# Two MoE layers behind a delta-rule attention: first loads reordered, expert 0 staged elsewhere, first pair split, order lists drawn

## The chip, the cores and the metric

One NeuronCore of a Trainium2 chip (trn2) runs the whole program. The metric is device time in microseconds (us) of that core. TensorE (PE) multiplies matrices, with weight loads (PEld) beside it; VectorE (DVE), ScalarE (ACT) and GpSimd (POOL) do the rest; the sync engine's queue (SP) issues nearly all transfers, which run on 16 DMA engines.

## The reference, cut to what matters

```python
def _attn_ref(q, k, v, beta):
    k_n = k / (np.linalg.norm(k, axis=-1, keepdims=True) + 1e-06)
    for t in range(S):
        y[:, :, t] = np.einsum('bhd,bhde->bhe', q[:, :, t], state)
        v_old = np.einsum('bhde,bhd->bhe', state, kt)
        state = state + bt[:, :, :, None] * np.einsum('bhd,bhe->bhde', kt, vt - v_old)

def _moe_ref(x, w_gate, w1, w2):
    P = np.exp(logits - logits.max())
    for _ in range(8):
        P /= P.sum(1, keepdims=True) + 1e-09
        P /= P.sum(0, keepdims=True) + 1e-09
        P *= N / E
    for e in range(E):
        out += P[:, e:e + 1] * (np.maximum(x @ w1[e], 0.0) @ w2[e])
```

Attention is a delta rule over 768 steps for 4 batches of 8 heads of 48. Its output, 3072 tokens of 384, goes through a dense MoE layer (8 experts, 384 to 1024 to 384, each token weighted by a Sinkhorn-normalised matrix), and then through a second MoE layer in which each token goes to one expert only.

## The kernel before, in words

Attention is done in 24 blocks of 64 steps (`block(i)`, L517; block i is chunk i // 2 of batch pair i % 2). A block loads its keys and queries (`KQ`) and values in node `ld` (L561 to L566), squares and normalises the keys (L568 to L605), inverts a triangular 64x64 matrix per head in five levels `z`, `a` (L673 to L687), applies the running state (L710 to L757) and writes its output, split into a high and a low f16 half and transposed, into a ring `xring` (nodes `px`, `xe`, L796 to L806). Every f32 operand is split in that way, and each product takes three f16 matmuls.

Two blocks give 256 tokens, on which `moe_unit(e, r)` (L828) runs expert 0, and half of expert 1, of the first MoE layer: a first layer (L851), relu and split (L862, L864), a second layer (L877) and a store through `yo` (L887). Unit (0, r) has 72 matmuls of 256 columns and 48 of 384; unit (1, r) has half of each. `seq` fixes the order of the units: (0,0), (0,1), (1,0), (0,2), (1,1) and so on. A unit's first matmul waits for the output of both its blocks and for the end of the unit before.

Weights come as f32 and are split on the chip by `prep_nodes` (L911): loads `wl` (L933), a Square over them on ACT to find a scale (`wa`, L946), and the splits `we` on ACT (L984) and `wf` on DVE (L986). Expert 0 is staged in `xring` before the ring has data: first `w1` in three loads; then, when all its splits are done, `w2` in one load to the same place. The gate weights have a chain of their own (`wg0` to `wg`, L1035 to L1051). Zero tiles for the block-diagonal operands of the first blocks are loaded from HBM (L1059).

What sets the order of all this is a planner, `Sched` (L45). Every piece of work is a node with an engine, a cost, dependencies and a priority; `run` (L91) simulates the engines and issues at each step the ready node that can start first, the lowest priority number first among those that can. A result counts as seen on another engine `HOP` ns later (3000 for a DMA, plus the node's `lat`); `floor` is the earliest time of a node in the simulation. Each engine then works through its list strictly in that order. A node's priority in a block is `fpr`, i minus a lead (L432, L559); block 2's front has -1, block 3's 0, block 1's 1. The last stage (routing, and the second MoE layer's queue) is ordered by the same class.

One `KQ` buffer serves all blocks but block 1, whose keys lie in `hhl`; so `ld` of block i waits until block i-1 has used its keys (block 2: block 0):

```python
N("ld", "D", 1300, f, [("kl", pb), ("ql", pb), ("kn", pb), P4("r2l"), P4("sqv")]
  if i > 1 else [("cs", 0), ("wl02", 0)] if i else [])
```

After the attention stage PE goes on with the other experts (from L1263), then routing, then the second MoE layer.

Of the kernel before, what the change touches and what calls it, by code (L numbers as in the profile page):

```python
# [7 lines left out]
F32 = mybir.dt.float32  # L8
# [36 lines left out]
class Sched:  # L45
    HOP = {"P": 200.0, "V": 135.0, "A": 150.0, "G": 100.0, "D": 3000.0}
# [4 lines left out]
    SLACK = 300.0  # L51

# [38 lines left out]
    def run(self):  # L91
        ready = [n for n in self.nodes if n.wait == 0]
        left = len(self.nodes)
        while left:
            best = None
            per = {}
            for n in ready:
                opt = None
                for e, c_ in n.alts:
                    s = self.start(n, e)  # L100
                    if s is None:
                        continue
                    w = s + c_ + (self.BIAS.get(e, 0.0) if not n.one else 0.0)
                    if opt is None or w < opt[3]:
                        opt = (s, e, c_, w)
                if opt:
                    per.setdefault(opt[1], []).append((opt[0], n.prio, n, opt[2]))
            for e, cs_ in per.items():
                lim = max(self.free[e], min(x[0] for x in cs_)) + 1.0
                if e == "P":  # L110
                    mo = [x for x in cs_ if x[2].moe]
                    at = [x for x in cs_ if not x[2].moe]
                    if mo and at:
                        adv = self.free["P"] - self.tlast
                        self.tlast = self.free["P"]
                        self.credit = min(self.credit + adv * SH0, 1500.0)
                        ta = min(x[0] for x in at)
                        tm = min(x[0] for x in mo)
                        now = self.free["P"]
                        cs_ = mo if (self.credit >= 400 and tm <= max(now, ta) + 50) or (ta > now + 100 and tm < ta - 50) else at  # L120
                        lim = max(self.free[e], min(x[0] for x in cs_)) + 1.0
                x = min((y for y in cs_ if y[0] <= lim), key=lambda y: (y[1], y[0]))
                if best is None or x[0] < best[0]:
                    best = (x[0], e, x[3], x[2])
            s, e, c_, n = best
            if e == "P":
# [18 lines left out]
            n.fn(*args)  # L145
            end = s + c_
            self.free[e] = end
            self.log.append((n.name, e, s, end))
            if n.holder is not None:
                h = n.holder  # L150
                h.left -= 1
                h.fin = max(h.fin, end + self.FREE)
                if h.left == 0:
                    self.slots[h.ps[0]][h.slot] = h.fin
            ready.remove(n)
            left -= 1
            for m in n.out:
                m.wait -= 1
                same = e == "P" and m.one and m.alts[0][0] == "P"
                slack = self.SLACK + self.TOP[e] if m.one and m.alts[0][0] == "P" and not same else 0.0  # L160
                m.ready = max(m.ready, end + (0.0 if same else self.HOP[e]) + n.lat + slack)
                if m.wait == 0:
                    ready.append(m)


@with_exitstack
def kernel(
# [58 lines left out]
    lg = res.tile([128, NT, E], F32, name="lg")  # L226
# [18 lines left out]
    P = P9[:, :, 0:E]  # L245
    pet = res.tile([128, E + 1, NT], F32, name="pet")
# [188 lines left out]
    LP, AP, SP = 0.03, 0.7, 1.7  # L435
# [6 lines left out]
    with (  # L442
# [74 lines left out]
        def block(i):  # L517
# [21 lines left out]
            def front(name, shape, dt, at):  # L539
# [266 lines left out]
            N("xe", (("A", 690), ("V", 480)), 0, f, ["px", "W0", ("W1a", i // 4), ("mo", (i // 2) - NXR), ("x1", i - 2 * NXR - 1 + i % 2)], frees="px", prio=tp)  # L806
# [21 lines left out]
        def moe_unit(e, r):  # L828
# [13 lines left out]
            XR = xring[:, r % NXR]  # L842
            for g4 in range(nf // per):
                for j in range(per):
                    f_ = per * g4 + j
                    for kk in range(KD):
                        def f(slot=None, g4=g4, j=j, f_=f_, kk=kk):
                            if j == 0 and kk == 0:
                                o[g4] = ps1.tile([128, 512], F32, name="pt")
                            for x, (wv, xv) in enumerate(((0, 0), (0, 1), (1, 0))):  # L850
                                nc.tensor.matmul(  # L851
                                    out=o[g4][:, 256 * j:256 * j + 256], lhsT=w1v(W, wv, kk, f_), rhs=XR[:, xv, kk],
# [7 lines left out]
                        N(nm, "P", 327, f, dep, ps=("pt", 1) if j == 0 and kk == 0 else None, cols=768, moe=True)  # L860
# [7 lines left out]
            for j, t_ in enumerate(blks):  # L868

                spare = j % 2 and t_ >= NT - 5  # L870
                for f_ in range(nf):
                    def f(slot=None, j=j, f_=f_, spare=spare):
                        if f_ == 0:
                            o["py", j] = pyt(slot if spare else None)
                        c_ = 256 * (f_ % per) + 128 * j
# [35 lines left out]
        def prep_nodes(e, W, st, prio, deps, wdeps, hf=None, iv=None, fro=True):  # L911
# [5 lines left out]
            for x, wsrc in enumerate((moe_w1, moe_w2)):  # L917
                o = {}
                so = 0
                if hf is None:  # L920
# [9 lines left out]
                else_ = deps[x] if hf is not None and (x == 0 or so) else pv  # L930
                lof = {}
                for n_, (cs_, dst, src) in enumerate(loads):
                    Q((f"wl{x}{n_}", iv), "D", 650, lambda dst=dst, src=src: nc.sync.dma_start(out=dst, in_=src),  # L933
                      deps[n_] if x == 0 and hf is None else else_, prio[x][0], lat=1500.0 if len(cs_) < NCH else 4500.0, floor=4500.0)
                    for c in cs_:
                        lof[c] = (f"wl{x}{n_}", iv)
                if fro:

                    wd_ = 1024 if hf is None else 768
                    np_ = len(cks) * CW // wd_  # L940
                    for n_ in range(np_):
                        def f(n_=n_, o=o, so=so, x=x, wd_=wd_, np_=np_):
# [3 lines left out]
                            nc.scalar.activation(out=jk, in_=st[:, so + n_ * wd_:so + n_ * wd_ + wd_], func=AF.Square, accum_out=o["mx"][:, n_:n_ + 1])  # L946
# [34 lines left out]
                for n_, c in enumerate(cks):  # L981
                    a, b = so + n_ * CW, so + n_ * CW + CW
                    h_, l_ = (W[:, wcol(x, c, part):wcol(x, c, part) + CW] for part in range(2))
                    Q((f"we{x}{n_}", iv), "A", 520, lambda a=a, b=b, h_=h_, o=o: nc.scalar.activation(  # L984
                        out=h_, in_=st[:, a:b], func=AF.Copy, scale=o["s"]), [(f"wd{x}", iv)] + wdeps[x], prio[x][2])
                    Q((f"wf{x}{n_}", iv), "V", 602, lambda a=a, b=b, h_=h_, l_=l_, o=o: nc.vector.scalar_tensor_tensor(  # L986
                        out=l_, in0=st[:, a:b], scalar=o["s"], in1=h_, op0=ALU.mult, op1=ALU.subtract), [(f"we{x}{n_}", iv)], prio[x][2])
# [47 lines left out]
        Q(("wg0", 0), "D", 650, lambda: nc.sync.dma_start(out=wg_s, in_=moe_w_gate.rearrange("(k p) e -> p k e", p=128)), [("bt2", 0)], 0.6)  # L1035
# [5 lines left out]
        Q(("wg1", 0), "V", 90, f, [("wg0", 0)], 0.6)  # L1041

        pmax("wg2", 0, lambda: wgo["m"], wgo, 0.6, [("wg1", 0)])
# [4 lines left out]
        Q(("wg3", 0), "V", 700, f, [("wg2", 0)], 0.6)  # L1048
        Q(("wg4", 0), "A", 220, lambda: nc.scalar.activation(out=wgh, in_=wg_s, func=AF.Copy, scale=wgo["s"]), [("wg3", 0)], 0.6)
        Q(("wg", 0), "V", 150, lambda: nc.vector.scalar_tensor_tensor(  # L1050
            out=wgl, in0=wg_s, scalar=wgo["s"], in1=wgh, op0=ALU.mult, op1=ALU.subtract), [("wg4", 0)], 0.6)  # L1051
# [14 lines left out]
        w0a, w0 = prep_nodes(0, W0, xring.rearrange("p r a k n -> p (r a k n)").bitcast(F32), [(LP, AP, SP), (WP, WP, WP)], [[]] * 3, [[], []])  # L1066
# [7 lines left out]
        for i in range(NT):  # L1074
            block(i)
            if i % 2:
# [59 lines left out]
        sch.run()  # L1136
# [678 lines left out]
```

## Time and profile before

| | |
|---|---|
| three timed runs | 2177.27 us median (2176.48 to 2181.3) |
| the profiled execution | 2180.33 us, span 2178.6 us |
| mean granted clock of PE | 0.975 |
| PE / DVE / ACT / POOL busy | 2040.0 / 1217.7 / 837.5 / 265.6 us |
| MoE weight loads into `st`, the largest group of transfers | 28 of 1536 KB |

Times in the rows are us from the start of the span. "Idle before" is the time that the engine stood still just before an instruction, with what ended it. A granted clock of 1.00 is PE's upper level, 0.50 the lower. One execution was profiled; the runs of the table were timed without a profile.

### The profile page before, as it was taken

The numbers are of one execution on the slowest core, as the hardware profiler recorded it, in microseconds if no ns is written. First come the engines' busy times: TensorE is split into PE (matmuls) and PEld (weight loads), VectorE is DVE, ScalarE is ACT, GpSimd is POOL, SyncE is SP. The second block draws the span as 40 slices with busy tenths as digits, with TensorE's granted clock in tenths as the row PEclk, the third lists the DMA queues.
The fourth block names the chain that finished last, engine by engine and source line by source line (L and its number), as shares of the span: only waits on it lengthen the run. The fifth ranks groups of instructions, "written<-read, shape, count | busy, mean of one in ns | idle before, by whom it ended". The sixth has DMA issues, their size and how long they took to land. (4 is left out here: it accounts for less than half of the span.)

```text
span 2178.6 us, 45252 instructions
## 1 busy us (share of the span) xinstructions
PE 2040.0 (94%) x18968; PEld 1290.2 (59%) x18968; DVE 1217.7 (56%) x2777; ACT 837.5 (38%) x1568; POOL 265.6 (12%) x301
## 2 busy tenths in 40 slices
PE   3689988988998989999999999999999999999999
PEld 3567777777775435555555555555555555557776
DVE  6889888877872564555455455554552245552111
ACT  6666655565542332232222222222231135443332
POOL 3232233222200000000000000000000000113221
PEclk9589999999999999999999999999999999999999
DMA  7345555555534233113203113212300001058765
GB/s 263 85 100 110 118 108 102 113 110 105 131 100 167 95 99 116 59 59 116 87 30 116 59 65 110 88 48 99 116 30 1 1 16 29 23 187 318 253 235 205
DMA packets 328321, 232.51 MB, mean 107 GB/s; under 512 B 258908, under 2 KB 305920, under 8 KB 321714
## 3 DMA queue, kind: packets, MB, share of 16 engines
q1 hardware_dynamic: 322674, 217.76, 34.1%
q0 software_dynamic: 4288, 10.25, 1.3%
q8 instruction: 150, 2.46, 0.5%
q10 hardware_dynamic: 1152, 1.57, 0.2%
q14 instruction: 57, 0.47, 0.1%
HBM read 148.51 MB, written 51.93 MB: 92 GB/s over the span
## 5 line engine op out<-in xcount | busy, mean ns | idle before, releaser
L355 PE MATMUL pt<-big,W 128*128 128x512 f16 x2304 | 507.1, 380 | 9.4 <-DVE hhl L339 5.8
L355 PEld LDWEIGHTS <-W 128*128 128x128 f16 x2304 | 225.9, 98 | 280.6 <-issue 14.9
L366 PE MATMUL py<-W,hhl 128*128 128x384 f16 x1632 | 286.8, 327 | 4.1 <-DVE accb L385 3.9
L366 PE MATMUL py<-W,ttb 128*128 128x384 f16 x1440 | 253.6, 326 | 0.0
L338 ACT ACTIVATE hhl<-pt 128x512 f16<-128x512 f32 x136 | 81.1, 596 | 412.8 <-PE pt L355 412.1
L366 PEld LDWEIGHTS <-hhl 128*128 128x128 f16 x1632 | 160.0, 98 | 115.0 <-issue 6.7
L366 PEld LDWEIGHTS <-ttb 128*128 128x128 f16 x1440 | 140.9, 98 | 93.1
L385 DVE SCALAR_TENSOR_TENSOR accb<-py,pet,accb 128x384 f32<-128x384 f32 x136 | 83.9, 617 | 185.9 <-PE py L366 184.2
L851 PE MATMUL pt<-xring,W 128*128 128x256 f16 x1296 | 177.7, 275 | 0.5 <-DVE hhl L864 0.5
L339 DVE SCALAR_TENSOR_TENSOR hhl<-pt,hhl 128x512 f16<-128x512 f32 x136 | 93.9, 690 | 147.5 <-ACT hhl L338 147.4
L877 PE MATMUL py<-W,hhl 128*128 128x384 f16 x756 | 152.9, 331 | 6.3 <-ACT yo L887 3.8
L339 DVE SCALAR_TENSOR_TENSOR ttb<-pt,ttb 128x512 f16<-128x512 f32 x120 | 83.0, 691 | 108.4 <-ACT ttb L338 108.4
L338 ACT ACTIVATE ttb<-pt 128x512 f16<-128x512 f32 x120 | 71.6, 597 | 151.4 <-PE pt L355 151.4
L298 DVE TENSOR_REDUCE wmx<-st 128x1 f32<-128x512 f32 x168 | 109.8, 677 | 33.9 <-DMA st<-in_moe_w_dram 33.9
L305 POOL PARTITION_ALL_REDUCE wma<-wm x28 | 10.1, 362 | 945.5 <-DVE wm L303 945.5
L851 PEld LDWEIGHTS <-W 128*128 128x128 f16 x1296 | 114.7, 99 | 15.3 <-issue 0.6
L1327 PEld LDWEIGHTS <-W 128*128 128x128 f16 x1008 | 91.1, 98 | 53.7 <-issue 2.6
L1347 PE MATMUL py<-W,hhl 128*128 128x384 f16 x624 | 108.8, 326 | 0.0
L877 PEld LDWEIGHTS <-hhl 128*128 128x128 f16 x864 | 76.0, 99 | 46.9 <-issue 5.9
L1327 PE MATMUL pt<-big,W 128*128 128x512 f16 x432 | 97.6, 379 | 1.4 <-DVE hhl L1333 1.2
L1333 DVE SCALAR_TENSOR_TENSOR ttb<-pt,ttb 128x512 f16<-128x512 f32 x50 | 34.6, 692 | 111.5 <-ACT ttb L1332 111.1
L502 DVE TENSOR_TENSOR Z<-pz,cs 128x512 f16<-128x512 f32 x120 | 80.3, 674 | 10.3 <-PE pz L488 9.9
(373 smaller groups left out, 3094.0 us busy)
## 6 DMA issues: line engine op xcount, KB each, us to landing
st<-in_moe_w_dram SPq DMA_DIRECT2D x28, 1536.0 KB, 9.6
W<-w2d SPq DMA_DIRECT2D x18, 1536.0 KB, 8.7
w2d<-big SPq DMA_DIRECT2D x16, 1536.0 KB, 6.2
big<-w2d SPq DMA_DIRECT2D x8, 1536.0 KB, 7.1
accb<-w2d SPq DMA_DIRECT2D x8, 1536.0 KB, 8.4
big<-kqc SPq DMA_DIRECT2D x90, 128.0 KB, 3.8
KQ<-in_kq_dram SPq DMA_DIRECT2D x23, 448.0 KB, 4.8
st<-PTc SPq DMA_DIRECT2D x42, 128.0 KB, 2.7
```

The source lines that it names most:

```text
L298: nc.vector.tensor_reduce(out=mx[:, c:c + 1], in_=st[:, c * CW:c * CW + CW], op=ALU.max, axis=AX.X, apply_absolute_value=True)
L338: nc.scalar.activation(out=oh, in_=pt, func=AF.Relu)
L339: nc.vector.scalar_tensor_tensor(out=ol, in0=pt, scalar=0.0, in1=oh, op0=ALU.max, op1=ALU.subtract)
L355: nc.tensor.matmul(out=po, lhsT=lhsT, rhs=rhs, start=(i == 0), stop=(i == 3 * KD - 1))
L366: nc.tensor.matmul(out=py[:, 0:DM], lhsT=lhsT, rhs=rhs, start=(n == 0), stop=(n == 3 * (KF - fs) - 1))
L385: nc.vector.scalar_tensor_tensor(out=acc[t], in0=py[:, 0:DM], scalar=pe[x][:, t:t + 1], in1=acc[t], op0=ALU.mult, op1=ALU.add)
L502: ENG[e].tensor_tensor(out=out, in0=in0, in1=in1, op=op)
L851: nc.tensor.matmul(out=o[g4][:, 256 * j:256 * j + 256], lhsT=w1v(W, wv, kk, f_), rhs=XR[:, xv, kk], start=(kk == 0 and x == 0), stop=(kk = ...
L877: nc.tensor.matmul(out=o["py", j][:, 0:DM], lhsT=a_[f_ // per][:, c_:c_ + 128], rhs=w2v(W, b_, f_), start=(f_ == 0 and x == 0), stop=(f_ = ...
L1327: nc.tensor.matmul(out=po, lhsT=w1v(W, wv, kk, f), rhs=xv[:, kk, :], start=(kk == 0 and x == 0), stop=(kk == KD - 1 and x == 2))
L1333: V((f"rs{q_}", id_), lambda q_=q_: nc.vector.scalar_tensor_tensor(out=HL[q_], in0=o[q_], scalar=0.0, in1=HH[q_], op0=ALU.max, op1=ALU.sub ...
L1347: nc.tensor.matmul(out=o["py"][:, 0:DM], lhsT=a_[f // per][:, c_:c_ + 128], rhs=w2v(W, b_, f), start=(f == 0 and x == 0), stop=(f == KF - ...
```

## The change

The loads of the first blocks are moved in SP's list: block 1's waits for the constants only, block 3 gets a key buffer that is free from the start (two `KQ` buffers, by the block's parity), and from block 4 on `ld` waits for block i-2. Expert 0's `w1` loads get a later floor (9 us in the simulation) and a lower priority; its `w2` is staged in two halves in the parts of expert 1's tile `W1` that hold nothing yet, so it doesn't wait for the splits of `w1`. Block output into the ring waits for the splits of `w1` only. The first pair of blocks is given to the MoE layer as two units of one block (128 columns each). The gate weights' chain gets priority 1.4. The logits `lg` are written into the tile of the probabilities. The planner separates the plan from the issue, draws 40 plans with shuffled priorities, replays each six times with random delays (`late`), and issues the best; its DMA hop is 3400. The last stage's `run()` draws once.

```diff
@@
-    HOP = {"P": 200.0, "V": 135.0, "A": 150.0, "G": 100.0, "D": 3000.0}
+    HOP = {"P": 200.0, "V": 135.0, "A": 150.0, "G": 100.0, "D": 3400.0}
+    SHUFFLE = 0.2
-    def run(self):
+    def run(self, draws=1):
+        base = [(n.prio, n.wait, n.ready) for n in self.nodes]
...
+        for k in range(draws):
+            rng = random.Random(k)
+            for n, (p, w, r) in zip(self.nodes, base):
+                n.prio, n.wait, n.ready = p + (self.SHUFFLE * (rng.random() - 0.5) if k and p < 1e5 else 0.0), w, r
...
+            order = self.plan()
+            if order is None:
+                continue
+            end = sum(self.late(order, random.Random(j)) for j in range(6)) if draws > 1 else 0.0
+            if best is None or end < best[0]:
+                best = (end, order, self.log)
...
+    def late(self, order, rng):
...
+                if de != "P" or e != "P":
+                    t += self.HOP[de] + d.lat + 80.0 * rng.random() + (1000.0 * rng.random() ** 2 if de == "D" else 0.0)
...
+            elif rng.random() < 0.06:
+                c_ += 200.0 + 400.0 * rng.random()
...
+        return max(free.values())
+
+    def plan(self):
...
-    lg = res.tile([128, NT, E], F32, name="lg")
+    lg = P
...
-    LP, AP, SP = 0.03, 0.7, 1.7
+    LP, AP, SP = 0.35, 0.7, 1.7
...
-                return tl(name, shape, dt, 0)
+                return tl(name, shape, dt, key)
...
-                t = front("KQ", [896], F32, 0)
+                t = front("KQ", [896], F32, 0, par)
-            N("ld", "D", 1300, f, [("kl", pb), ("ql", pb), ("kn", pb), P4("r2l"), P4("sqv")] if i > 1 else [("cs", 0), ("wl02", 0)] if i else [])
+            N("ld", "D", 1300, f, ([] if i == 3 else [("kl", i - 2), ("ql", i - 2), ("kn", i - 2)]) + [P4("r2l"), P4("sqv")] if i > 1 else [("cs", 0)] if i else [], lat=500.0, **(dict(prio=0.15) if 0 < i < 3 else {}))
...
-            N("xe", (("A", 690), ("V", 480)), 0, f, ["px", "W0", ("W1a", i // 4), ("mo", (i // 2) - NXR), ("x1", i - 2 * NXR - 1 + i % 2)], frees="px", prio=tp)
+            N("xe", (("A", 690), ("V", 480)), 0, f, ["px", ("W0a", 0), ("W1a", i // 4), ("mo", (i // 2) - NXR), ("x1", i - 2 * NXR - 1 + i % 2)], frees="px", prio=tp)
...
-        def moe_unit(e, r):
+        def moe_unit(e, r, only=None):
...
-            blks = [2 * r, 2 * r + 1]
+            blks = [2 * r, 2 * r + 1] if only is None else [2 * r + only]
+            nt_ = 128 * len(blks)
+            c0 = 128 * (only or 0)
...
-            per = 2
+            per = 512 // nt_
...
-            XR = xring[:, r % NXR]
+            XR = xring[:, r % NXR, :, :, c0:c0 + nt_]
...
-                        N(nm, "P", 327, f, dep, ps=("pt", 1) if j == 0 and kk == 0 else None, cols=768, moe=True)
+                        N(nm, "P", 327 if nt_ == 256 else 170, f, dep, ps=("pt", 1) if j == 0 and kk == 0 else None, cols=3 * nt_, moe=True)
...
-                        (cks, st.rearrange("p (k f) -> p k f", k=KF), wsrc[e].rearrange("(k p) f -> p k f", p=128))]
+                        (cks[KD * u:KD * u + KD], st1[u].rearrange("p (k f) -> p k f", k=FH), wsrc[e][512 * u:512 * u + 512].rearrange("(k p) f -> p k f", p=128))
+                        for u in range(2)]
...
-                else_ = deps[x] if hf is not None and (x == 0 or so) else pv
+                else_ = deps[x] if hf is not None and (x == 0 or so) else pv if st1 is None else []
...
-                      deps[n_] if x == 0 and hf is None else else_, prio[x][0], lat=1500.0 if len(cs_) < NCH else 4500.0, floor=4500.0)
+                      deps[n_] if x == 0 and hf is None else else_, prio[x][0], lat=1500.0, floor=9000.0 + 6000.0 * x)
...
-        Q(("wg0", 0), "D", 650, lambda: nc.sync.dma_start(out=wg_s, in_=moe_w_gate.rearrange("(k p) e -> p k e", p=128)), [("bt2", 0)], 0.6)
+        Q(("wg0", 0), "D", 650, lambda: nc.sync.dma_start(out=wg_s, in_=moe_w_gate.rearrange("(k p) e -> p k e", p=128)), [("bt2", 0)], 0.5, lat=4000.0)
...
-        w0a, w0 = prep_nodes(0, W0, xring.rearrange("p r a k n -> p (r a k n)").bitcast(F32), [(LP, AP, SP), (WP, WP, WP)], [[]] * 3, [[], []])
+        w0a, w0 = prep_nodes(0, W0, xring.rearrange("p r a k n -> p (r a k n)").bitcast(F32), [(LP, AP, SP), (LP, AP, WP)], [[]] * 3, [[], []],
+                             st1=[W1[:, 6144 * u:6144 * u + 3072].bitcast(F32) for u in range(2)])
...
-            if i % 2:
+            if i < 2:
+                moe_unit(0, 0, i)
+            elif i % 2:
                 moe_unit(0, i // 2)
...
-        sch.run()
+        sch.run(40)
```

## Rows read from the trace of the kernel before

**Rows 1.** The page's 40 slices of the span, busy tenths.

```profile
PE   3689988988998989999999999999999999999999
...
DVE  6889888877872564555455455554552245552111
```

**Rows 2.** Windows: stretch, length, busy PE PEld DVE ACT POOL, PEclk, DMA, GB/s.

```profile
0.00:160.00 160.00, 95.89 (x1662) 82.42 (x1664) 125.90 (x328) 106.31 (x224) 50.31 (x52) 0.80 0.56 148
160.00:620.00 460.00, 421.87 (x7883) 335.74 (x7880) 380.09 (x880) 269.31 (x563) 123.03 (x109) 0.98 0.54 112
620.00:720.50 100.50, 91.36 (x614) 59.06 (x612) 38.81 (x104) 25.40 (x45) 1.34 (x6) 0.95 0.37 128
720.50:2178.00 1457.50, 1430.88 (x8822) 813.01 (x8819) 672.92 (x1466) 436.45 (x737) 90.89 (x134) 0.99 0.28 99
```

**Rows 3.** Timeline (start, length, engine): Sinkhorn's end, the next stage's first matmuls.

```profile
659.11 0.24 DVE L426 TENSOR_SCALAR pet<-pet,ivt 128x24 f32<-128x24 f32 x1
...
720.50 4.05 PE L355 MATMUL pt<-big,W 128*128 128x512 f16 x18
```

**Rows 4.** Windows inside the first 124 us.

```profile
10.00:20.00 10.00, 4.93 (x46) 4.71 (x46) 4.40 (x10) 5.12 (x9) 1.45 (x2) 1.00 1.02 334
20.00:30.00 10.00, 1.81 (x26) 1.63 (x27) 3.83 (x13) 6.30 (x15) 1.15 (x1) 1.00 0.78 266
...
80.00:124.00 44.00, 31.58 (x641) 28.47 (x641) 37.41 (x92) 29.73 (x61) 13.75 (x12) 0.61 0.37 75
```

**Rows 5.** Timeline of SP, the first 42 us.

```profile
10.79 0.33 SPq L564 DMA_DIRECT2D KQ<-in_kq_dram  x1
...
15.31 5.69 SPq L1059 DMA_DIRECT2D ttb<-in_zer_dram  x1
...
21.52 0.48 SPq L564 DMA_DIRECT2D hhl<-in_kq_dram  x1
...
41.19 0.38 SPq L933 DMA_DIRECT2D xring<-in_moe_w_dram  x1
```

**Rows 6.** Timeline, 20 to 28 us; idle before in brackets.

```profile
20.87 0.63 ACT L577 ACTIVATE K<-KQ 128x512 f16<-128x512 f32 x1 [5.69 <-DMA KQ<-in_kq_dram]
...
23.91 0.18 DVE L1040 TENSOR_REDUCE wm<-wg_s 128x1 f32<-128x24 f32 x1 [5.74 <-DMA wg_s<-in_moe_w_gate_dram]
...
26.09 0.52 ACT L570 ACTIVATE K<-hhl 128x384 f32<-128x384 f32 x1 [2.77 <-DMA hhl<-in_kq_dram]
...
27.85 0.59 PE L488 MATMUL pz<-t,W 128*128 128x64 f16 x8 [9.90 <-ACT W L506]
```

**Rows 7.** DMA, first 50 us: packets; zero fills, KB, us to landing.

```profile
DMA packets 9807, 14.01 MB, mean 280 GB/s; under 512 B 4940, under 2 KB 6732, under 8 KB 9804
...
big<-in_zer_dram SPq DMA_DIRECT2D x9, 512.0 KB, 9.1
```

**Rows 8.** Timeline of PE: output of blocks 0 and 1, first MoE matmuls.

```profile
79.20 0.83 PE L799 MATMUL px<-c,yhl 128*128 128x128 f16 x6
...
122.25 0.49 PE L799 MATMUL px<-c,yhl 128*128 128x128 f16 x6 [0.41 <-DVE mx L780]
...
124.24 1.80 PE L851 MATMUL pt<-xring,W 128*128 128x256 f16 x15
```

**Rows 9.** Timeline of PE: matmuls of 128, 256 and 384 columns.

```profile
140.67 1.50 PE L657 MATMUL pg<-kqc,big 128*128 128x128 f16 x24
...
648.68 4.09 PE L851 MATMUL pt<-xring,W 128*128 128x256 f16 x36
...
658.10 4.06 PE L877 MATMUL pz<-W,hhl 128*128 128x384 f16 x24
```

**Rows 10.** Waits, 160 to 620 us: total us, times, longest.

```profile
ACT K L570 <- DMA KQ<-in_kq_dram: 26.9, 14, 5.0
...
DVE ss L582 <- ACT K L570: 12.5, 8, 4.0
...
PE sv L592 <- DVE ss L584: 5.7, 3, 3.7
```

More of the change, by code (lines that the diff above doesn't have):

```diff
@@ L1 @@
+import random
 from contextlib import ExitStack
@@ L89, in start @@
         return s
-    def run(self):
+    def run(self, draws=1):
+        base = [(n.prio, n.wait, n.ready) for n in self.nodes]
+        free, slots = dict(self.free), {k_: list(v) for k_, v in self.slots.items()}
+        best = None
+        for k in range(draws):
+            rng = random.Random(k)
+            for n, (p, w, r) in zip(self.nodes, base):
+                n.prio, n.wait, n.ready = p + (self.SHUFFLE * (rng.random() - 0.5) if k and p < 1e5 else 0.0), w, r
+            self.free, self.slots = dict(free), {k_: list(v) for k_, v in slots.items()}
+            self.warm, self.tick, self.colsum, self.credit, self.tlast, self.log = False, 0, 0.0, 0.0, 0.0, []
+            order = self.plan()
[4 more added lines that the diff above has]
+                best = (end, order, self.log)
+        self.log = best[2]
+        for n, e, slot, c_, args in best[1]:
+            n.slot = slot
+            n.fn(*args)
@@ new lines, in late @@
+    def late(self, order, rng):
+        ends, free, place, left, fin = {}, dict.fromkeys("PVAGD", 0.0), {}, {}, {}
+        warm, tick, cols = False, 0, 0.0
+        for n, e, slot, c_, _ in order:
+            r = 0.0
+            for d in n.deps:
+                de, t = ends[d]
+                if de != "P" or e != "P":
+                    t += self.HOP[de] + d.lat + 80.0 * rng.random() + (1000.0 * rng.random() ** 2 if de == "D" else 0.0)
+                r = max(r, t)
+            if n.ps:
+                r = max(r, place.get((n.ps[0], slot), 0.0))
+                left[n], fin[n] = n.ps[1], (n.ps[0], slot)
+            b = max(r, free[e])
+            if e == "P":
+                while b >= (tick + 1) * self.TICK:
+                    warm = cols >= 3060
+                    tick += 1
+                    cols = 0.0
+                c_ = c_ if warm else c_ * 2 - 20
+                cols += n.cols
+            elif rng.random() < 0.06:
+                c_ += 200.0 + 400.0 * rng.random()
+            free[e] = b + c_
+            ends[n] = (e, b + c_)
+            if n.holder is not None:
+                h = n.holder
+                left[h] -= 1
+                place[fin[h]] = max(place.get(fin[h], 0.0), b + c_ + self.FREE)
+        return max(free.values())
@@ L92, in run @@
+    def plan(self):
+        order = []
         ready = [n for n in self.nodes if n.wait == 0]
@@ L124, in run @@
                     best = (x[0], e, x[3], x[2])
+            if best is None:
+                return None
             s, e, c_, n = best
+            cost = c_
             if e == "P":
@@ L144, in run @@
                 args.append(e)
-            n.fn(*args)
+            order.append((n, e, getattr(n, "slot", None) if n.ps else None, cost, args))
             end = s + c_
@@ L163, in run @@
                     ready.append(m)
+        return order
 @with_exitstack
@@ L537, in block, with front @@
             par = i % 2
-            def front(name, shape, dt, at):
+            def front(name, shape, dt, at, key=0):
                 if i == 1:
@@ L851, in f @@
                                 nc.tensor.matmul(
-                                    out=o[g4][:, 256 * j:256 * j + 256], lhsT=w1v(W, wv, kk, f_), rhs=XR[:, xv, kk],
+                                    out=o[g4][:, nt_ * j:nt_ * j + nt_], lhsT=w1v(W, wv, kk, f_), rhs=XR[:, xv, kk],
                                     start=(kk == 0 and x == 0), stop=(kk == KD - 1 and x == 2),
@@ L919, in prep_nodes, with at @@
                 so = 0
+                def at(a, b, x=x):
+                    return st[:, a:b] if x == 0 or st1 is None else st1[a // 1536][:, a % 1536:(b - 1) % 1536 + 1]
                 if hf is None:
@@ L937, in prep_nodes, with f @@
                 if fro:
-                    wd_ = 1024 if hf is None else 768
+                    wd_ = 1024 if hf is None and x == 0 else 768
                     np_ = len(cks) * CW // wd_
                     for n_ in range(np_):
-                        def f(n_=n_, o=o, so=so, x=x, wd_=wd_, np_=np_):
+                        def f(n_=n_, o=o, so=so, x=x, wd_=wd_, at=at):
                             if n_ == 0:
@@ L945, in f @@
                             jk = W[:, 6144 * x:6144 * x + wd_]
[L946 removed]
+                            nc.scalar.activation(out=jk, in_=at(so + n_ * wd_, so + n_ * wd_ + wd_), func=AF.Square, accum_out=o["mx"][:, n_:n_ + 1])
                         Q((f"wa{x}{n_}", iv), "A", 190 + 1.04 * wd_, f, sorted({lof[cks[y]] for y in range(n_ * wd_ // CW, -(-(n_ + 1) * wd_ // CW))}) + (
@@ L983, in prep_nodes @@
                     h_, l_ = (W[:, wcol(x, c, part):wcol(x, c, part) + CW] for part in range(2))
[L984 to L987, printed above, removed]
+                    Q((f"we{x}{n_}", iv), "A", 520, lambda a=a, b=b, h_=h_, o=o, at=at: nc.scalar.activation(
+                        out=h_, in_=at(a, b), func=AF.Copy, scale=o["s"]), [(f"wd{x}", iv)] + wdeps[x], prio[x][2])
+                    Q((f"wf{x}{n_}", iv), "V", 602, lambda a=a, b=b, h_=h_, l_=l_, o=o, at=at: nc.vector.scalar_tensor_tensor(
+                        out=l_, in0=at(a, b), scalar=o["s"], in1=h_, op0=ALU.mult, op1=ALU.subtract), [(f"we{x}{n_}", iv)], prio[x][2])
                     pv.append((f"wf{x}{n_}", iv))
@@ L1047, in f @@
             nc.vector.tensor_copy(out=ivg, in_=p2g)
-        Q(("wg3", 0), "V", 700, f, [("wg2", 0)], 0.6)
-        Q(("wg4", 0), "A", 220, lambda: nc.scalar.activation(out=wgh, in_=wg_s, func=AF.Copy, scale=wgo["s"]), [("wg3", 0)], 0.6)
+        Q(("wg3", 0), "V", 700, f, [("wg2", 0)], 1.4)
+        Q(("wg4", 0), "A", 220, lambda: nc.scalar.activation(out=wgh, in_=wg_s, func=AF.Copy, scale=wgo["s"]), [("wg3", 0)], 1.4)
         Q(("wg", 0), "V", 150, lambda: nc.vector.scalar_tensor_tensor(
-            out=wgl, in0=wg_s, scalar=wgo["s"], in1=wgh, op0=ALU.mult, op1=ALU.subtract), [("wg4", 0)], 0.6)
+            out=wgl, in0=wg_s, scalar=wgo["s"], in1=wgh, op0=ALU.mult, op1=ALU.subtract), [("wg4", 0)], 1.4)
         def f():
```

8 lines of the change are left out of this document (4 added, 4 removed).

## The prediction

> **What bounds the kernel now.** I read the page's row of 40 slices first. TensorE (PE) is nearly full in every slice except the first six or so, and VectorE (DVE) is full just there [rows 1]. The windows by stage put numbers on it. Up to 160 us PE is busy 95.89 of 160 (64.1 idle). From 160 to 620, while the 24 attention blocks run woven with the first MoE layer, 421.87 of 460 (38.1 idle). To 720.5, 9.1 idle. In the whole rest 26.6 of 1457.5 [rows 2]. So after the start the kernel is bound by PE, and nearly half of all idle PE time lies in the first 160 us. A microsecond taken out of the start moves everything behind it, because the work behind it is PE work without slack. The last routing step of that layer (Sinkhorn) ends at 659 while PE is busy with MoE work until 720.5, so an earlier end of attention doesn't run into it [rows 3].
>
> What bounds the start is seen in the finer windows, the sync queue (SP) and the idle columns. Between 10 and 30 us DVE does 8.2 us of work, from 80 to 124 it does 37.41 of 44, and PE's granted clock is 0.61 there on the mean, mostly the lower of its two levels, 1.2 of 2.4 GHz [rows 4]. So the early stretch waits, and what it leaves undone fills DVE later. The waits have names: SP issued block 2's keys at 10.79, then stood 5.69 us in one zero fill, and sent block 1's keys only at 21.52 [rows 5]. ScalarE (ACT), which takes its list in order, sat 5.69 us for block 2's keys and 2.77 us for block 1's; DVE sat 5.74 us for the gate weights; PE got its next matrices after 9.90 us [rows 6]. The 16 DMA engines had moved 14.01 MB in the first 50 us, 280 GB/s on the mean [rows 7]. Block 0's output reaches PE at 79.2, block 1's only at 122.25, and the first MoE matmul, which waits for both, at 124.24 [rows 8].
>
> **Part by part.**
> *Loads of the first blocks ahead.* Block 1 no longer waits for the third weight load, block 3 waits for nothing (it has its own key buffer), the weights of expert 0 go behind them in SP's order, and the gate weights' DVE work goes behind block 1. Removed: the two ACT waits, 5.69 + 2.77 = 8.46 us. DVE's 5.74 and PE's 9.90 lie in the same 15 to 28 us and aren't added. Bounds: nothing, if other loads take their place; 11.8 at most (20 minus 8.2, DVE's idle time in that stretch). I take **8.5**, because ACT's rows are the ones that held the other two engines. Moved past: block 3's two loads now go before the constants, 640 KB, at 280 GB/s 2.3 us on the queue; against it the beta load is rid of the 1.5 MB of weights ahead of it. Taken at nothing, between 2.3 lost and 3.1 won (1.5 MB less 0.64 MB at that rate). The gate weights are needed first by block 0's logits, after its output at 79.2 [rows 8], so 50 us of other work cover their delay.
>
> *Expert 0's second layer in expert 1's tile.* Its load no longer waits for the first layer's splits: in the old list that load left at 41.19 [rows 5]. One load becomes two (0.38 us of SP more). Nothing read it before 124, so by itself it is worth **0**; it is what lets a unit start before that. Were its cover gone, it would cost what is in rival 3.
>
> *First pair block by block.* Unit (0,0) becomes two units. The second layer's matmuls are the same 48, and ACT and DVE get the same four groups of 512 columns. In the first layer 72 matmuls of 256 columns become 144 of 128. The rows: 36 of 256 columns take 4.09 us, 0.114 each; 24 of 128 columns, each with its own weights, take 1.50, 0.0625 each (both with the drain of the last one) [rows 9]. 144 x 0.0625 - 72 x 0.114 = 9.0 - 8.2 = **0.8 lost**. The Trainium skill (TensorE: Matmul & The Clock Gate, section Back-to-back issue gap) speaks against this part: it gives about 81 ns for each matmul of 128 columns in a stream of weight loads and matmuls. By that it would be 11.7 us and 3.5 lost, and the sum below 2.7 us smaller; the row here, 62.5 ns at most, disagrees with it, and the row decides.
> What it brings: half a unit, 72 x 0.0625 + 24 matmuls of 384 columns in 4.06 = 8.6 us of PE work at the full clock, can start once block 0's output is there, in a stretch where PE is idle 12.4 us [rows 4, 9]. Bounds 0 and 8.6: if PE runs out of MoE work again behind it, the time is only idle later. Unit (0,0) began 2.0 us after block 1's output [rows 8], so PE had no MoE work in store there, and DVE, which makes that work ready, is near full. I take **4**, the middle.
>
> *Two key buffers.* The keys of block i now load when block i-2 is done with them, not i-1. ACT waited for them 14 times from 160 to 620, 26.9 us; behind that DVE waited 12.5 us for ACT's squares and PE 5.7 us [rows 10]. Between 0 (PE gets its idle time elsewhere) and 12.5 I take **6**, nearest to PE's own row, as PE is the bound.
>
> *Shuffled lists and the new DMA hop of 3400.* Forty orders are planned with priorities shifted by up to 0.1, and the one with the earliest end in the planner's own noisy replay is issued. This acts on 38.1 us of PE idle time [rows 2]; no row shows another list. Bounds 8 gained and 8 lost, a fifth of that. I take **0**. The last stage's list changes by the hop only: PE idles 26.6 us in all behind 720.5 and I keep 2 either way. Writing the logits into the probabilities' tile changes no instruction's size: 0.
>
> Sum: 8.5 - 0.8 + 4 + 6 = **17.7 us**. The profiled execution took 2180.33 (span 2178.6), so it would take 2162.6; it is 3.1 over the median of 2177.27, hence 2159.6 for a median. I say **2160**.
>
> **Rivals.**
> 1. *All of it pays.* PE fills the whole 12.4 us, DVE's 12.5 is won and the list is better: 11.8 + 8.6 + 12.5 + 8 - 0.8 = 40, 2137. For it: with the granted clock at 0.61 from 80 to 124, PE's steps of the attention chain are long there, and MoE matmuls between them could bring the clock up sooner. Against: DVE's 37.41 of 44 in that stretch leaves little [rows 4].
> 2. *Only a little moves.* DVE is what binds up to 124, so the early waits return as later ones, PE gets no gain from the keys: 4 to 0 us, 2173 to 2177. For it: DVE's 37.41 of 44 us just ahead of the first unit, whose instructions all stay. Against: 8.2 of 20 us busy is a hole that blocks with their keys in place can fill.
> 3. *Slower: the weights come late and ACT stands at them.* In the old list the weight loads left right behind block 0's. Now they are planned from 9 us on (the second layer's from 15), the planner counts 4.9 us to their landing, and the zero fills lie around them on full DMA engines; those took 9.1 us [rows 7]. 4.2 us short, on each of five loads (three and two), and each in ACT's order ahead of block 1 and 2: 21 us of waits in place of 8.46, 12.5 lost; the early unit gives nothing (0.8 lost), the key buffers perhaps 6: 2184, and 2190 without them. It decides if three or more of the five loads hold ACT (two give 8.4, what was there before). Against: loads of one queue land in a row, so one wait covers most of the next.
> 4. *It doesn't do what it says.* If the unshuffled draw wins, the list is the planner's own, and only the last 0 of the sum is concerned; 2160 stands.
>
> **How the numbers follow.** My forecast, 2148 to 2171, 0.60; rival 1, under 2148, 0.12; rival 2, 2171 to 2182, 0.17; rival 3, above 2182, 0.11. About 0.2% (4.4 us) is what a measurement of this kernel can tell from no change: under 2172.9 is faster, above 2181.6 slower. From rival 2 a share of 0.03 falls below 2172.9: faster 0.75, same 0.14, slower 0.11. The range 2145 to 2179 leaves out most of rivals 1 and 3, about 2 in 10, and holds the sum with key buffers and early loads each at nothing as well as with the upper values of two of them.
>
> **What would show it.** Right: block 1's squares begin before 15 us, ACT has no wait over 3 us between 10 and 30, the first MoE matmul stands at 70 to 90 with 128 columns, PE idles about 50 instead of 64.1 us up to 160 and about 32 instead of 38.1 from 160 to 620, ACT's waits for keys fall to a few us. Wrong: ACT waits for weight loads between 15 and 35 (rival 3), block 1's output still comes near 120 (rival 2), or PE's idle time from 160 to 620 is above 45, the list being worse than the old one; then the sum's last two terms were wrong.

## The result and the profile after

The changed kernel took 2158.22 us (median of five, 2156.3 to 2165.27) against 2177.27 (five runs, 2176.07 to 2181.3): a ratio of 0.9916, 95% interval 0.9901 to 0.9932. That is faster by more than 0.2%, and 1.8 us from the 2160 that was forecast. Its profiled execution took 2156.3 (span 2154.5). That the time was right is half of the answer only: the terms behind it were mostly not, as the parts below show.

First the page's slices of the kernel after, which answer to [rows 1].

```profile
PE   3779999999998889999999999999999999989998
...
DVE  6988988987771755445455555555442255551111
```

PE is at nine tenths or more in slices 4 to 12, where before has four at eight tenths; slice 13 (646 to 700 us) now holds the change of stages. The windows of the kernel after by stage (columns as in [rows 2], which they answer to, and [rows 4] for the last three) give the amounts. The next stage now begins at 694.62 instead of 720.50 [rows 3].

```profile
0.00:160.00 160.00, 101.90 (x1835) 88.20 (x1836) 132.87 (x346) 110.56 (x232) 44.54 (x49) 0.90 0.59 155
160.00:620.00 460.00, 434.30 (x7967) 344.32 (x7965) 386.41 (x913) 275.68 (x573) 118.00 (x110) 0.99 0.56 116
...
0.00:694.60 694.60, 602.10 (x10222) 474.02 (x10223) 543.52 (x1319) 402.29 (x834) 162.54 (x158) 0.97 0.55 127
694.60:2154.50 1459.90, 1430.02 (x8822) 812.49 (x8819) 672.62 (x1466) 436.38 (x737) 90.94 (x134) 1.00 0.28 99
...
10.00:20.00 10.00, 4.10 (x42) 3.86 (x42) 7.01 (x20) 5.96 (x14) 2.77 (x4) 1.00 0.93 295
20.00:30.00 10.00, 2.85 (x42) 2.51 (x43) 8.64 (x28) 7.98 (x17) 4.50 (x4) 1.00 1.01 386
80.00:124.00 44.00, 38.32 (x840) 32.88 (x838) 40.94 (x113) 33.46 (x70) 11.27 (x11) 0.92 0.44 97
```

PE's idle time fell from 64.1 to 58.1 us up to 160, and from 38.1 to 25.7 from 160 to 620. Up to the first matmul of the next stage it fell from 111.4 (720.5 less 609.1 busy) to 92.5 (694.6 less 602.1): 18.9 us. PE's busy time fell by 7.0, for which the prediction had no term. The rest behind 694.6 takes 1.8 more than before (1459.9 to 1458.1). So 18.9 + 7.0 - 1.8 = 24.1, the difference of the spans. The medians differ by 19.05, because before's profiled execution lay 3.1 above its median and after's 1.9 below. Two thirds of the idle time won, 12.4 us, lies in the middle, not at the start.

The timeline of the kernel after (start, length, engine, in brackets the idle time before and what ended it) answers to [rows 6, 8, 9].

```profile
12.86 0.52 ACT L631 ACTIVATE K<-hhl 128x384 f32<-128x384 f32 x1
...
33.10 0.84 ACT L1013 ACTIVATE W<-W 128x768 f16<-128x768 f32 x1 [1.79 <-DMA W<-in_moe_w_dram]
34.66 0.72 DVE L569 COPY big<-K 64x768 f16<-64x768 f16 x2 [3.88 <-DMA big<-in_zer_dram]
...
85.95 0.82 PE L860 MATMUL px<-c,yhl 128*128 128x128 f16 x6
87.66 2.50 PE L914 MATMUL pt<-xring,W 128*128 128x128 f16 x42 [0.37 <-ACT xring L567]
112.64 0.50 PE L860 MATMUL px<-c,yhl 128*128 128x128 f16 x6
```

Block 1's keys are squared at 12.86, and ACT's waits of 5.69 and 2.77 us are gone; its longest between 8 and 45 us is 2.05. Of rival 3's sign two short waits for weights are there, 1.15 us at 25.46 and 1.79 at 33.10. The DMA engines are as full as before, 14.30 MB in the first 50 us at 286 GB/s, as in [rows 7]. And a new wait has come up: DVE, 3.88 us, for zero tiles. Block 0's output comes 6.75 us later than before (85.95 after 79.20), block 1's 9.6 earlier (112.64 after 122.25). The first MoE matmul comes at 87.66 with 128 columns, as the change says.

The waits of the kernel after from 160 to 620 (us in total, times, longest) answer to [rows 10].

```profile
ACT K L631 <- DMA KQ<-in_kq_dram: 8.5, 5, 3.6
ACT K L638 <- DMA KQ<-in_kq_dram: 1.3, 2, 1.1
...
PE sv L653 <- DVE ss L645: 1.9, 2, 1.0
```

ACT's waits for keys fell from 26.9 us to 9.8, PE's for the norms from 5.7 to 1.9.

### The profile page after: what moved, and what is told of

Same layout as the page of the kernel before. It is cut to its first block, busy times and chain, and to the rows that moved or that the text cites. A ratio compares the mean times of both kernels' runs of the same rounds, so it can differ in the third digit from the quotient of the medians.

```text
span 2154.5 us, 45362 instructions
## 1 busy us (share of the span) xinstructions
PE 2032.1 (94%) x19042; PEld 1286.5 (60%) x19042; DVE 1216.1 (56%) x2785; ACT 838.7 (39%) x1571; POOL 253.5 (12%) x292
## 5 line engine op out<-in xcount | busy, mean ns | idle before, releaser
L914 PE MATMUL pt<-xring,W 128*128 128x256 f16 (+1 forms) x1368 | 179.6, 270 | 3.6 <-ACT xring L567 1.8
```

The source lines that it names most:

```text
L914: nc.tensor.matmul(out=o[g4][:, nt_ * j:nt_ * j + nt_], lhsT=w1v(W, wv, kk, f_), rhs=XR[:, xv, kk], start=(kk == 0 and x == 0), stop=(kk = ...
```

## The experiments

All the runs of one group below were compared with runs of the kernel before on the same chip (medians 2178.11 us for e1 to e4, 2180.54 for e5 to e8, 2178.69 for e9 to e11 and 2178.63 for e12). The change itself was measured against 2177.27. So runs of different groups are better compared by their ratios than by their times. Stage ends and idle times come from one profiled execution of each kernel.

### One part at a time

**e1: the change without the draw.** The planner's own list is issued, as before the change.

```diff
-        sch.run(40)
+        sch.run(1)
```

> The changed kernel with one plan, the unshuffled one, in place of the best of forty. Theory A (the prediction: early loads, early unit, key buffers; the drawn list is worth nothing): 2158 to 2164, PE idle from 160 to 620 still near 26 us. Theory B (the drawn list is most of the gain): the planner's own replay puts this list's end 17 us later than that of the list it chose (699.5 against 682.5), so 2168 to 2176, with PE idle from 160 to 620 back near 36 us.

Measured: 2165.06 us (2161.11 to 2168.72), ratio 0.9934 [0.9913, 0.9955]. The next stage begins at 703.65; PE idles 61.1 us up to 160 and 25.9 from 160 to 620. The draw is worth 6 to 7 us on top of the other parts, though this interval touches that of the whole change.

**e2: the draw alone.** The kernel before, with the new planner (40 lists, replay), nothing else; the DMA hop stays 3000.

```diff
+    SHUFFLE = 0.2
...
-        sch.run()
+        sch.run(40)
```

> The kernel before, with nothing changed but the planner: forty shuffled plans, replayed, the best issued (hop still 3000). Theory A: no gain, 2173 to 2181, since the stalls of the first 30 us and the key waits stay. Theory B: the replay sees 8 us (689.1 for the old list, 680.8 for the best), so about 2169, or less if the replay understates; PE idle from 160 to 620 below 32 us, the start unchanged.

Measured: 2158.15 us (2150.05 to 2160.69), ratio 0.9900 [0.9877, 0.9923]. This is the whole gain with none of the other parts. It has one key buffer, the old loads and no split unit. Its windows (columns as in [rows 2]):

```profile
0.00:160.00 160.00, 103.03 (x1837) 88.43 (x1839) 136.13 (x351) 111.02 (x233) 51.24 (x54) 0.77 0.60 156
160.00:620.00 460.00, 431.23 (x7924) 342.88 (x7923) 391.28 (x917) 276.16 (x575) 107.24 (x101) 1.00 0.54 117
```

PE idles 57.0 us up to 160, less than with the new loads (58.1), and 28.8 from 160 to 620.

**e3: two key buffers alone.** The kernel before with the second `KQ` buffer, one plan. (The logits go into the probabilities' tile, which makes the room.)

```diff
-                t = front("KQ", [896], F32, 0)
+                t = front("KQ", [896], F32, 0, par)
...
-    [("kl", pb), ("ql", pb), ("kn", pb), P4("r2l"), P4("sqv")] if i > 1
+    ([] if i == 3 else [("kl", i - 2), ("ql", i - 2), ("kn", i - 2)]) + [P4("r2l"), P4("sqv")] if i > 1
```

> The kernel before with two key buffers (keys of block i wait for block i-2, block 3 for nothing; logits in the probabilities' tile to make room), one unshuffled plan, all else as before. Theory A: 6 us off, about 2171, ACT's waits for keys from 160 to 620 down from 26.9 to under 8 us. Theory B: any list is a draw with a spread of some 6 us in the replay, so between 2165 and 2187 with no relation to the key waits, which may well vanish without a gain.

Measured: 2159.29 us (2156.06 to 2162.72), ratio 0.9907 [0.9886, 0.9927]; next stage at 703.4, PE idle 61.5 and 30.0. This part alone also gives the whole gain, yet its waits for keys from 160 to 620 (us in total, times, longest) are far from gone:

```profile
ACT K L570 <- DMA KQ<-in_kq_dram: 17.3, 7, 4.2
```

That is 17.3 of the 26.9 us there were. Two parts give 20 and 19 us alone, and together with the others 19. So the gains don't add, and e3 gains twice the 9.6 us by which its waits for keys shrank. Any edit of the graph also makes the planner write another list, which led to the theory that the old list was a poor one, and that any other list gains most of it.

**e4: the change with the first pair as one unit,** 40 draws.

```diff
-            if i < 2:
-                moe_unit(0, 0, i)
-            elif i % 2:
+            if i % 2:
```

> The changed kernel with the first pair as one unit of 256 columns again (forty draws as in the change). Theory A: 3 us lost, 2161; PE idle from 80 to 124 back up by 4 to 8 us. Theory B: the replay's best end is 681.5 here against 682.5, so no loss, 2153 to 2160.

Measured: 2154.29 us (2152.82 to 2156.37), ratio 0.9884 [0.9865, 0.9904], 3.9 below the whole change, with overlapping intervals. The split brings nothing that can be seen. The windows from 80 to 160 of this kernel say why it looked good:

```profile
80.00:124.00 44.00, 30.41 (x594) 27.16 (x594) 40.56 (x99) 27.23 (x57) 11.76 (x11) 0.67 0.42 94
124.00:160.00 36.00, 34.19 (x651) 28.36 (x648) 34.14 (x88) 24.65 (x52) 11.81 (x11) 0.98 0.65 120
```

The same window behind it in the kernel after:

```profile
124.00:160.00 36.00, 28.06 (x523) 23.74 (x521) 29.73 (x78) 20.22 (x46) 9.13 (x10) 0.76 0.61 109
```

With the split PE is busy 38.32 us from 80 to 124 at a granted clock of 0.92, without it 30.41 at 0.67. From 124 to 160 it is the other way round, 28.06 at 0.76 with the split and 34.19 at 0.98 without. So up to 160 both idle the same, 58.1 and 57.9 us: the work that fills the hole is missing later. The two kernels also follow different lists, so this is not the split alone.

### The list, with everything else held

**e5, e6, e9: the kernel before with another list each** (the lists of draws 10, 9 and 32, not the best one), and **e7, e10: the kernel after with the lists of draws 30 and 39.** The edit is one line in the planner, here for e5:

```diff
-        for k in range(draws):
+        for k in (10,) if draws > 1 else (0,):
```

> The kernel before with one fixed shuffled list, draw 10, whose replay end (697.8) is the mean of the draws and 8.7 us behind the old list's (689.1). Theory C (the old list is by chance a bad one on the chip, and nearly any other list is better): 2158 to 2172. Theory B (the replay ranks lists rightly): slower than before, 2183 to 2190. Theory A' (the old order of loads holds the start, lists are worth little): 2173 to 2183.

> The kernel before with draw 9, the worst in the replay (713.4, 24 us behind the old list and 33 behind the best). Theory C with a replay that ranks at all: 2175 to 2190, clearly worse than draw 10. Theory B: 2195 to 2205. If the replay ranks nothing: like draw 10.

> The changed kernel with draw 30, the worst of its forty in the replay (710.4 against 682.5 of the one it issues and 699.5 of the unshuffled one, which took 2165 on the chip). If the replay ranks rightly: 2172 to 2186. If not: 2155 to 2168, as the other lists of this structure.

> The kernel before with draw 32 (replay end 698.4, the mean of its draws). With draw 10 (697.8) this makes two lists of mean rank with the old loads, one key buffer and the pair together. If these parts cost what the prediction says (17.7 us): at least 2172. If the old list alone was bad: near draw 10, 2158 to 2170.

> The changed kernel with draw 39 (replay end 699.8, the mean of its draws; the unshuffled one has 699.5 and took 2165). Two lists of mean rank with the new loads, two key buffers and the split pair. If these parts are worth 17.7 us at equal rank: 2145 to 2155. If they are worth little: 2160 to 2170, the same as the two of the kernel before.

e9 came out as expected if the parts count (at least 2172), e10 as expected if they are worth little (2160 to 2170), and e7 between its two ranges; these forecasts decide nothing.

The second column is the planner's own replay of the attention stage, no time of the chip. The last two give the waits for keys from 160 to 620, and PE's idle time up to 160 and from there to 620.

| kernel, list | replay | median us | ratio and interval | next stage at | key waits | PE idle |
|---|---|---|---|---|---|---|
| before, old list | 689.1 | 2177 to 2181 | 1 | 720.5 | 26.9 | 64.1, 38.1 |
| before, draw 34 (e2) | 680.8 | 2158.15 | 0.9900 [0.9877, 0.9923] | 692.0 | 15.1 | 57.0, 28.8 |
| before, draw 10 (e5) | 697.8 | 2163.39 | 0.9921 [0.9907, 0.9935] | 701.0 | 6.4 | 63.4, 26.1 |
| before, draw 32 (e9) | 698.4 | 2176.99 | 0.9993 [0.9979, 1.0007] | 714.9 | 8.4 | 60.1, 34.4 |
| before, draw 9 (e6) | 713.4 | 2182.83 | 1.0015 [1.0004, 1.0026] | 720.6 | 12.6 | 59.7, 35.9 |
| after, draw 38 (the change) | 682.5 | 2158.22 | 0.9916 [0.9901, 0.9932] | 694.6 | 9.8 | 58.1, 25.7 |
| after, own list (e1) | 699.5 | 2165.06 | 0.9934 [0.9913, 0.9955] | 703.7 | 9.0 | 61.1, 25.9 |
| after, draw 39 (e10) | 699.8 | 2160.53 | 0.9915 [0.9895, 0.9935] | 699.9 | 10.8 | 66.6, 24.3 |
| after, draw 30 (e7) | 710.4 | 2169.87 | 0.9948 [0.993, 0.9966] | 709.2 | 9.7 | 59.8, 31.7 |

Five things follow.

Lists of the same work on the kernel before span 25 us, 2158 to 2183. That is more than the whole change.

The theory that any other list gains is wrong: draws 9 and 32 gain nothing. But the old list is one that the replay misjudges. It promised 689 and the stage ended at 720.5, 31 later; the other lists end between 1 earlier and 17 later than promised.

The waits for keys don't go with the time or with the buffer. Draw 10 has one key buffer and waits 6.4 us, less than the change with two:

```profile
ACT K L638 <- DMA KQ<-in_kq_dram: 3.5, 4, 1.7
...
ACT K L631 <- DMA KQ<-in_kq_dram: 2.9, 4, 2.4
```

What goes with the end of the stage is PE's idle time in the middle (24 to 29 us in the rows whose stage ends by 704, 32 to 38 in the others). Up to 160 there is no such order: 57 to 67 in the former, 60 to 64 in the latter.

Idle time is only part of it. On the kernel before, with the same 10148 matmuls up to the next stage, PE's busy time there is 598.1 us in e2, 602.7 in e5, 609.1 with the old list, 611.2 in e9 and 614.3 in e6. Of the 28.6 us between the ends of e2 and e6, 12.4 are idle time and 16.2 are busy time. PE's granted clock from 160 to 620 follows: 1.00, 0.99, 0.98, 0.97 and 0.97. How much of the busy time the clock explains was not isolated.

Lists that the replay ranks alike can be compared across the two kernels. Near 698 to 700, before took 2163.39 and 2176.99, mean 2170.2, and after 2165.06 and 2160.53, mean 2162.8. The edits to the graph are then worth some 7 us, or 6 when each run is compared with the kernel before in its own group. With 14 us between two lists of the same rank this is a rough figure, and nothing is not ruled out.

In e10 rival 3's wait is there. The waits of this kernel up to 160:

```profile
ACT W L1013 <- DMA xring<-in_moe_w_dram: 10.6, 3, 8.8
```

Three waits of ACT for expert 0's weights come to 10.6 us, and PE's idle time up to 160 is 66.6, the most in the table; that the one makes the other was not shown. The run was still 18.2 us faster than before.

### The loads

**e8: the change with the old order of the first loads,** 40 draws.

```diff
-    LP, AP, SP = 0.35, 0.7, 1.7
+    LP, AP, SP = 0.03, 0.7, 1.7
...
-  if i > 1 else [("cs", 0)] if i else [], lat=500.0, **(dict(prio=0.15) if 0 < i < 3 else {}))
+  if i > 1 else [("cs", 0), ("wl02", 0)] if i else [], lat=500.0)
...
-  lat=1500.0, floor=9000.0 + 6000.0 * x)
+  lat=1500.0, floor=4500.0)
```

> The changed kernel with the loads of the start in the old order (weights of expert 0 first, floor 4.5 us, block 1 behind the third of them), forty draws, all else as changed. Prediction's first term: 8.5 us lost, 2167, with ACT waiting 5 us or more for keys in the first 30 us. Theory B and C: only what the list is worth; the replay's best end is 694.3 against 682.5, but mean ends differ by 4.5 only, so 2158 to 2170.

Measured: 2168.19 us (2165.43 to 2169.84), ratio 0.9944 [0.993, 0.9957]. The time is 10.0 above the whole change, but the kernel before took 3.3 longer in this group too; the ratios differ by 0.28%, some 6 us, and the intervals touch. PE idles 67.3 us up to 160 (58.1 with the new loads) and 28.3 from 160 to 620, the next stage begins at 707.0, and ACT's waits for keys up to 160 are back:

```profile
ACT K L638 <- DMA KQ<-in_kq_dram: 10.9, 2, 6.0
```

But the best of these 40 lists is also worse in the replay, 694.3 against 682.5. Over the change's own lists in the table, 17 us of replay (682.5 to 699.5) are worth 2 to 7 us, so the 11.8 may be worth 2 to 5 of the 6. And e2 has the old loads and idles 57.0. The new order may help this graph, by 1 to 4 us as an estimate; it isn't needed for a short start.

### A stall that both kernels have

Where the first units of expert 1's second half begin, PE stands 8.0 us, before the change (first line) and after it (second):

```profile
705.87 7.00 PE L1113 MATMUL pt<-big,W 128*128 128x512 f16 x18 [8.02 <-DVE hhl L1118]
```

```profile
681.40 5.58 PE L1183 MATMUL pt<-big,W 128*128 128x512 f16 x18 [8.02 <-DVE hhl L1188]
```

In the timeline of e4 (start, length, engine, idle before):

```profile
671.77 4.05 PE L1181 MATMUL pt<-big,W 128*128 128x512 f16 x18
672.24 0.48 ACT L1201 COPY yo<-pz 128x384 f32<-128x384 f32 x1 [5.60 <-DMA y2d<-yo]
678.24 0.48 ACT L1201 COPY yo<-py 128x384 f32<-128x384 f32 x1 [5.52 <-DMA y2d<-yo]
681.51 0.48 ACT L1201 COPY yo<-pz 128x384 f32<-128x384 f32 x1 [2.79 <-DMA y2d<-yo]
682.44 1.09 ACT L1185 ACTIVATE hhl<-pt 128x512 f16<-128x512 f32 x2 [0.46 <-ACT yo L1201]
683.82 6.54 PE L1181 MATMUL pt<-big,W 128*128 128x512 f16 x18 [8.00 <-DVE hhl L1186]
```

ACT copies each result into the one tile `yo` and can't copy the next until the store of 192 KB has read it; it waits 5.6, 5.5 and 2.8 us for that here. ACT's next splits stand behind these copies, DVE behind the splits, PE behind DVE.

**e11: e4 with four store tiles** for each group of four results, three of them in a part of `big` that is free there.

```diff
-  ob = hp.tile([128, DM], F32, name="yo")
+  x_ = 2 * WCOLS - 2 * DM * (3 - t_)
+  ob = big[:, x_:x_ + 2 * DM].bitcast(F32) if t_ < 3 else hp.tile([128, DM], F32, name="yo")
```

> The changed kernel with the pair together (e4, 2154.3) and, in the last two groups of expert 1, four store buffers in place of the one (three in a part of the tile big that holds nothing any more). PE's stall of 8.0 us there, seen in before, after and most runs, is put down to ACT waiting for one buffer's store while 6 MB are loaded. If so the stall falls under 2 us and the time by 5 to 8 us, to 2146 to 2150. If the transfers themselves bind, the next layer waits instead: 2152 to 2156.

Measured: 2142.19 us (2141.23 to 2144.76), ratio 0.9832 [0.981, 0.9854], 12.1 below e4 and beyond the 5 to 8 that were expected. In the timeline of e11 the copies now follow PE's results two us apart, and the wait of 8.0 is gone:

```profile
665.98 0.48 ACT L1202 COPY big<-py 128x384 f32<-128x384 f32 x1 [1.35 <-PE py L1194]
667.93 0.48 ACT L1202 COPY big<-pz 128x384 f32<-128x384 f32 x1 [1.47 <-PE pz L1194]
669.88 0.48 ACT L1202 COPY big<-py 128x384 f32<-128x384 f32 x1 [1.47 <-PE py L1194]
671.63 7.93 PE L1181 MATMUL pt<-big,W 128*128 128x512 f16 x36
671.83 0.48 ACT L1202 COPY yo<-pz 128x384 f32<-128x384 f32 x1 [1.47 <-PE pz L1194]
```

In the traces every engine of e11 issues its instructions in e4's order (up to 2000 us), so here one edit is measured under one list. The next stage begins at 687.2 in place of 698.0. Of these 10.8 us, 8.0 are the stall, and 2.5 are the 18 matmuls behind it: in e4 they took 6.54 us at a granted clock of 0.60, while the 18 before the stall took 4.05 at 1.00. In e11 all 36 take 7.93. Up to 160 and from there to 620 the idle times of the two kernels differ by some 2 us each, in opposite directions (59.5 and 27.0 here). As the list is the same, that much is the difference between two executions, and smaller differences in the table above say nothing.

**e12: e11 with 300 draws.**

```diff
-        sch.run(40)
+        sch.run(300)
```

> e11 with the best of 300 draws in place of 40 (replay end 675.2 against 681.5). In the changed kernel's lists 28 us of replay were 12 us on the chip, so 0.4 of 6.3: 2 to 3 us, 2137 to 2142. If the replay ranks only the coarse differences: 2138 to 2150 without a direction.

Measured: 2137.01 us (2136.03 to 2138.95), ratio 0.9812 [0.9789, 0.9835]. PE idles 22.4 us from 160 to 620 and the next stage begins at 678.6. That is 5.2 below e11, where 2 to 3 were expected, with intervals that overlap. This version beats both kernels: 41.6 us under before, 21.2 under the change.

## Why the prediction was right or wrong

- *The bound.* "A microsecond taken out of the start moves everything behind it" doesn't hold from one list to another: e10 idles 66.6 us up to 160 and yet begins the next stage at 699.9, e6 idles 59.7 and begins it at 720.6. The two also differ in the middle (24.3 and 35.9 idle) and in busy time (600.6 and 614.3), so a long start is outweighed there; what one microsecond of it is worth under one list was not measured. The middle was said to be full; of the idle time, its 38.1 us are where the lists differ most.
- *Loads, 8.5.* The mechanism came as said: ACT's two waits are gone, and DVE does 15.7 us of work from 10 to 30 instead of 8.2. But idle PE time up to 160 fell by 6.0 with all the parts of the start together, for which 11.7 had been summed. Part of the waits returned as DVE's 3.88 for zero tiles, and block 0 ends 6.75 later. The 1 to 4 us that are left of e8's 6 fall short of the 8.5; in the old graph a better list needs none of it.
- *Split first pair, 4 less 0.8.* The early unit began at 87.66 and raised PE's busy time from 80 to 124, as forecast, but the lower bound was the right one: "if PE runs out of MoE work again behind it, the time is only idle later". e4 against the change looks just like that. The price per matmul was right: 42 of 128 columns took 2.50 us, 0.0595 each, where 0.0625 had been taken. By the Trainium skill's 81 ns (TensorE: Matmul & The Clock Gate, section Back-to-back issue gap) they would take 3.4 us, as an estimate; the trace disagrees. All 144 took 9.9 us, some of them below the full clock, where 9.0 had been summed.
- *Two key buffers, 6.* The size of the gain in the middle was read off a wait that belonged to one list. e5 has one buffer and 6.4 of the 26.9 us; e3 has two buffers, 17.3 us of it and gains 19. Neither the wait nor the number of buffers gave the price here.
- *Shuffled lists, 0.* This is the step that failed. "No row shows another list" was true, and the fifth of 38.1 us was too small a bound: the same work under other lists took 2158 to 2183 us, 20 below and some 3 above the old list. In the change as made the draw is worth 6 to 7 (e1), in the kernel before 20 (e2), where the list that it replaces is the worst judged of all.
- *The sum.* 17.7 forecast, 19.05 measured. That it met is luck in good part, owed to errors that cancel: the middle gave 12.4 us of idle time where 6 was taken, the start 6.0 where 11.7 was. So two of its signs failed: PE idles 58.1 up to 160 where about 50 was said, and 25.7 from 160 to 620 where about 32 was.
- *The rivals.* Rival 2's conditions came in part (block 1's output at 112.64, between 100 and 120; the early waits moved to DVE), its time did not. Rival 3's wait exists in e10, 10.6 us, and that kernel is still faster than before. Of rival 1 the clock came (0.61 to 0.92 from 80 to 124), not the time. Rival 4 didn't come: the change issues draw 38.
- *Still open.* How much of the change is its edits and how much its list: some 7 us by lists of like rank, 0 against e2. The staging of expert 0's second layer, the gate weights' chain and the hop of 3400 were not taken out singly. Also why PE's busy time fell by 7.0. In e2, with the same instructions and the same mean granted clock of 0.94 as before up to the next stage, it fell by 11.0 (598.1 from 609.1). The mean hides where the clock was low: from 160 to 620, where PE is nearly full, it is 1.00 in e2 and 0.98 in before, and 2% of the 421.87 us busy there is 8.4 us, an estimate. Up to 160 it is lower, though, 0.77 against 0.80. So the clock may explain most of the 11.0, which was not isolated.

## What to carry to other kernels

Where a planner writes the lists that engines follow strictly in order, an edit changes the list too, and one list against one list measures both at once; time several lists of each version before an edit is credited, and let the chip, not the replay alone, choose among the best. A wait named in the trace belongs to the list it was seen in, so price it by what PE loses, in idle time and in busy time, and look whether another list has it at all. Small stores through one tile are worth a look of their own: here three more tiles gave 12.1 us under an unchanged list, the change's edits perhaps 7.

## What was not expected

- Lists of the same instructions differ by 25 us (1.1%), and the planner's replay, which came within 17 us of the others' end of the stage, missed the old list's by 31.
- ACT waited 5.6 us for a store of 192 KB to leave its tile in one place and 1.96 in another some 20 us later (in the kernel after, before its copies into `yo`); more tiles, in the place of e4's stall, took 12.1 us off. The DMA engines are full in the first place (share 1.06, 385 GB/s from 660 to 670) and little used in the second (0.22, 79 GB/s from 690 to 700), but no run took those transfers away, so the reason was not isolated.
- Standing still cost PE more than the wait: behind the 8.0 us of e4, 18 matmuls took 6.54 us in place of 4.05, at a granted clock of 0.60.
- PE's granted clock in the stretch from 80 to 124 rose from 0.67 to 0.92 by the early unit (e4 and the change), and the time did not fall.
